# Half of batch 0's keys and queries by casting DMAs, its value globals by register DMAs, a new order of the first stage, and batch 1's data ahead of w_out

## Chip, core and metric

The kernel runs on one core of one Trainium2 chip. The metric is the device time of one execution in microseconds (us). Before the change four runs gave a median of 332.36 us (331.63 to 333.47).

## What is computed

A windowed attention with eight global tokens, and behind it a two-layer network with a squared ReLU. q, k, v are (8 batches, 8 heads, 576 tokens, 64), in fp32.

```python
scores = scale * np.matmul(q, k.transpose(0, 1, 3, 2))
mask = np.abs(pos[:, None] - pos[None, :]) <= 32
mask = mask | is_global[:, None] | is_global[None, :]
scores = np.where(mask, scores, -1000000000.0)
attn = softmax(scores)                       # per query
x = (attn @ v) as (4608 tokens, 512)
out = relu(x @ w_in) ** 2 @ w_out            # 512 -> 2048 -> 512
```

## The kernel before

**Tiles.** Two heads make a pair, so a batch has four pairs. Keys lie in five tiles of up to 120 tokens, each with the 8 global keys ahead of them (`kt`, 128 columns a tile); queries lie in four groups of 144 tokens, each followed by the 8 global queries (`qt`, 608 columns). A batch's queries are worked in two halves of 304 columns. For a pair and a half, PE computes scores for the tiles that the window touches, ACT the exponential (`weights`, L648), PE the weighted sum of values and the sum of weights (`outputs`, L672), ACT the reciprocal as exp(-ln) (`finish_outputs`, L704 and L705), and DVE the product into `xT` (L732), the network's input with features on partitions. The results of the global queries are put together in `global_outputs` and copied into their columns by `scatter` (L751), eight copies at positions that DVE reads from registers (`load_columns`, L741).

**Batch 0** is the start of the kernel, and its data have a way of their own. SP loads k and q pair by pair as fp32 (`fetch_tokens`, L107; tiles `stk`, `stq`), DVE or ACT casts them (`cast_tokens`, L449; tile `nat0k`, `nat0q`), PE transposes them with the identity and picks the global rows by a product with a one-hot matrix (`transposed`, L471 and L483), and DVE and ACT copy the results from PSUM to `kt` and `qt` (`tr_k`, `tr_q`, L493 to L510). The half-0 mask is built of a band (`ub`) and of row indicators (`rows`) by `mask_natural` (L250, L256), corrected at the global positions (`mask_globals_matmul`, L267; `mask_globals`, L284), and added to the scores as the first product of their PSUM group (`mask_added`, L292; `mask_first`, L625). Half 1 multiplies by the mask after the exponential (L652). GpSimd makes the constants (identity, band, token numbers) before it issues its first DMA (v, L114). The global rows of v for batch 0 come from v itself: a product with a one-hot matrix (`v_globals`, L457), an ACT copy (L459) and a DVE copy into row 0 to 7 of `vb[0]` (L460). Those of batches 1 and 2 are fetched by SP with DMAs at register addresses (`fetch_globals`, L375; tile `grows`), and put in place by `globals_in_place` (L382 to L385).

**Order.** Each engine works its instructions in the order of the program, which is written out by hand. After the index list (`indices`) and the one-hots come pair 0's transposes, then a loop in which pair i+1 is transposed before pair i's scores, with the exponential behind them; then the outputs of half 0 of all pairs; then half 1. `keep_warm(n)` puts n products of zeros (L201) into PE's order. From there the network's units are woven in: `take(n)` issues n of the units in a list. A unit of the first layer for a half of batch 0 (`mm1_half`, L543) is 8 products, a unit of the second (`mm2`, L587) is 4. `SCHED` says how many go where: h0 to h3 and p0 to p2 before batch 1, and three numbers for each pair of batch 1 (`unit`, L865: behind the scores, between the two output groups, at the end). Later batches have fixed numbers.

**DMA queues.** POOL's order is v of batch 0, w_in (L784, four DMAs), w_out (L799, four), k and q of batch 1 (cast on the way, tiles `natk`, `natq`), v of batch 1 (`fetch_values`), and then the scratch copies of batch 2 (L419), which SP transposes by DMA (L431). A POOL DMA waits for the one eight places ahead of it. SP's order is batch 0's k and q, then the 24 DMAs of `fetch_globals`, then the copies of `value_globals` (L440).

`SCHED` before:

```python
SCHED = dict(h0=0, w=4, h1=2, h2=2, h3=0, p0=3, p1=1, p2=2, b1=((2, 1, 2), (1, 1, 2), (1, 1, 2), (1, 1, 2)))
```

Of the kernel before, what the change touches and what calls it, by code (L numbers as in the profile page):

```python
# [17 lines left out]
KT = 120  # L18
NT = 5
# [23 lines left out]
SCHED = dict(h0=0, w=4, h1=2, h2=2, h3=0, p0=3, p1=1, p2=2, b1=((2, 1, 2), (1, 1, 2), (1, 1, 2), (1, 1, 2)))  # L43
# [4 lines left out]
def kernel(  # L48
# [63 lines left out]
    def fetch_values(b, x, hs=slice(0, H)):  # L112
        back = NG if b == 0 and x else 0
        pool.dma_start(  # L114
            out=vb[b][NG - back : NG + KN[x], x, 2 * hs.start : 2 * hs.stop : 2],
            in_=v[b, hs, x * KT - back : x * KT + KN[x]].rearrange("h s d -> s h d"),
        )

    act.dma_start(out=g64, in_=global_idx.unsqueeze(0))
    for hp in range(NHP):  # L120
        for nm in "kq":
            fetch_tokens(nc.sync, nm, 0, hp)
    act.preload_act_table_set("natural_log_exp_and_others")

# [6 lines left out]
    pidx = sbt("pidx", [P, 4], I32)  # L131
    nc.gpsimd.iota(pidx, pattern=[[0, 4]], base=0, channel_multiplier=1)
    icb = sbt("icb", [P, 4], I32)
    nc.gpsimd.iota(icb, pattern=[[2 * H * S, 4]], base=2 * H * S, channel_multiplier=0)
    ig = sbt("ig", [P, NG], FP32)
    nc.gpsimd.iota(
        ig, pattern=[[1, NG]], base=0, channel_multiplier=0, allow_small_or_imprecise_dtypes=True,
    )

    U0 = 48  # L140
    UN = 208
    ub = [sbt(f"ub{i}", [P, UN], FP16) for i in range(2)]
    nc.gpsimd.memset(ub[0], 1.0)
    for base, cu, cm in (
        (-8, 0, 1), (window + U0 - 8, -1, 1), (window - U0 + 8, 1, -1),
    ):
        nc.gpsimd.affine_select(
            out=ub[0], in_=ub[0], compare_op=ALU.is_ge, fill=0.0,
            base=base, pattern=[[cu, UN]], channel_multiplier=cm,
        )  # L150
    rows = sbt("rows", [P, 2], FP16)
    nc.gpsimd.memset(rows, 1.0)
    for col, base, cm in ((slice(0, 2), -8, 1), (slice(1, 2), KN[-1] + 7, -1)):
        nc.gpsimd.affine_select(
            out=rows[:, col], in_=rows[:, col], compare_op=ALU.is_ge, fill=0.0,
            base=base, pattern=[[0, col.stop - col.start]], channel_multiplier=cm,
        )
    nc.gpsimd.affine_select(
        out=ub[1], in_=ub[0], compare_op=ALU.is_ge, fill=0.0,
        base=KN[-1] + 7, pattern=[[0, UN]], channel_multiplier=-1,  # L160
    )

    tok = sbt("tok", [P, NT], FP32)
    nc.gpsimd.iota(
        tok, pattern=[[KT, NT]], base=-8, channel_multiplier=1,
        allow_small_or_imprecise_dtypes=True,
    )
    nc.gpsimd.affine_select(
        out=tok, in_=tok, compare_op=ALU.is_ge, fill=-1.0,
        base=-8, pattern=[[0, NT]], channel_multiplier=1,  # L170
    )
    tokp = sbt("tokp", [P, TJ], FP32)
    nc.gpsimd.iota(
        tokp, pattern=[[1, TJ]], base=0, channel_multiplier=TJ,
        allow_small_or_imprecise_dtypes=True,
    )
    identity = sbt("identity", [P, P], FP16)
    nc.gpsimd.memset(identity, 0.0)
    nc.gpsimd.affine_select(
        out=identity, in_=identity, compare_op=ALU.not_equal, fill=1.0,  # L180
        base=0, pattern=[[-1, P]], channel_multiplier=1,
    )
    for kt in kts:
        dve.memset(kt[:, 4, 8 + KN[4] : P], 0.0)
# [4 lines left out]

    def clear_tail(op, t):  # L190
        op(t[96:P, NT - 1, 0 : 2 * H : 2], 0.0)

    clear_tail(dve.memset, vb[0])
    for x in range(NT):
        fetch_values(0, x)
# [168 lines left out]
    grows = sbt("grows", [NG, 3, 2, H, D], FP32, bufs=2, tag="gt")  # L364
    grow = {nm: grows[:, i] for i, nm in enumerate("kqv")}
    g16s = {nm: sbt("g16s" + nm, [NG, 2, H, D], FP16) for nm in "kqv"}

    def fetch_globals():
        _, at = nc.values_load_multi_w_load_instructions(
            g32c[0:1, 0:NG], engines=[mybir.EngineType.SP], min_val=0, max_val=S - 1,  # L370
            skip_runtime_bounds_check_because="the values are clamped on the chip",
        )
        for nm in "kqv":
            for g in range(NG):
                nc.sync.dma_start(  # L375
                    out=grow[nm][g : g + 1],
                    in_=src[nm][1:3, :, ds(at[g], 1), :].rearrange("b h o d -> o b h d"),
                )
# [74 lines left out]
    def v_globals(hp, op1=None, op2=None):  # L453
        vs = vb[0][:, :, 4 * hp : 4 * hp + 4 : 2]
        gl = pst("mm", [P, 512])[0:NG, 0 : 2 * D]
        for t in range(NT):
            nc.tensor.matmul(gl, oh[:, t, :], vs[:, t], start=(t == 0), stop=(t == NT - 1))  # L457
        gvs = sbt("gvs", [NG, 2 * D], FP16, bufs=2)
        (op1 or act.copy)(out=gvs, in_=gl)  # L459
        (op2 or dve.tensor_copy)(  # L460
            out=vs[0:NG],
            in_=gvs.rearrange("p (h d) -> p h d", d=D).unsqueeze(1).to_broadcast((NG, NT, 2, D)),
        )

    def transposed(nm, i, tag):
        b, hp = divmod(i, NHP)
        tr = pst(tag, [P, 1024], FP16)
        for j in range(TJ):
            n = TP + NG if (b and j == TJ - 1) else TP
            if b == 0:  # L470
                nc.tensor.transpose(  # L471
                    tr[:, TP * j : TP * j + n], nat0[(nm, hp)][:, j, :], identity[0:n, 0:n]
                )
            for e in range(2) if b else ():
# [5 lines left out]
        if b == 0:  # L480
            gl = tr.bitcast(FP32)[:, 384 : 384 + NG]
            for j in range(TJ):
                nc.tensor.matmul(  # L483
                    gl, nat0[(nm, hp)][:, j, :], ohp[0:TP, j, :],
                    start=(j == 0), stop=(j == TJ - 1), skip_group_check=True,
                )
# [175 lines left out]
    def outputs(i, half, et, tag, wins, columns=False):  # L662
        b, hp = divmod(i, NHP)
        acc = pst(tag, [P, 2, 512])
# [3 lines left out]
        for n, (t, so, c0, w) in enumerate(wins[half] if columns else ()):  # L668
            o = c0 - half * BANKC
            for x in range(2):  # L670
                for e in range(2):
                    nc.tensor.matmul(  # L672
                        acc[D * e : D * e + D, x, o : o + w],
# [3 lines left out]
        for e in () if columns else range(2):  # L677
            for n, (t, so, c0, w) in enumerate(wins[half]):
# [3 lines left out]
                    acc[:, e, o : o + w], vtf[:, t, vo : vo + P], et[:, e, so : so + w],  # L682
                    start=(n == 0), stop=(n == nw - 1), skip_group_check=True,
                )
        return acc
# [12 lines left out]
    def finish_outputs(i, half, acc, columns=False):  # L698
        b, hp = divmod(i, NHP)
        parts = PARTS[columns]  # L700
        av = acc[:, :, 0:BANKC].rearrange("p x (k c) -> p x k c", c=GRP)
        rec = sbt("rec", [P, 2, GTOK], FP32, bufs=2)
        for r, x, rs, xs in parts:
            act.activation(out=rec[r], in_=av[rs, xs, :, 0:GTOK], func=AF.Ln)  # L704
        act.activation(out=rec, in_=rec, func=AF.Exp, scale=-1.0)  # L705
        if b == 0:
            if half == 0:
                if hp == 0:
                    gsum[0] = sbt("gs", [P, NHP, 2, NG], FP32, bufs=2)
                dve.tensor_reduce(  # L710
                    out=gsum[0][:, hp], in_=av[:, :, :, GTOK:GRP].rearrange("p e k g -> p e g k"),
                    axis=AX.X, op=ALU.add,
                )
# [3 lines left out]
        else:  # L717
            if hp == 0 and half == 0:
                gsum[b] = sbt("gsh", [P, 2, NHP, 2, NG], FP32, bufs=2)
            dve.tensor_reduce(  # L720
                out=gsum[b][:, half, hp], in_=av[:, :, :, GTOK:GRP].rearrange("p e k g -> p e g k"),
                axis=AX.X, op=ALU.add,
            )
# [7 lines left out]
        for r, x, rs, xs in parts:  # L731
            dve.tensor_tensor(  # L732
                out=xT[r, hp, x0 : x0 + HS].rearrange("p (k x) -> p k x", k=2),
                in0=av[r, x, :, 0:GTOK], in1=rec[r], op=ALU.mult,
# [25 lines left out]
    def transposes0(hp):  # L760
# [3 lines left out]
    index_base()  # L764
    keep_warm(6)
    mask_natural(0)
    gb = indices()
    fetch_globals()
    keep_warm(4)
    one_hots(gb)  # L770
    act.copy(
        out=vb[0][0:NG, 0, 0 : 2 * H : 2], in_=idle[0:NG].rearrange("p (h d) -> p h d", d=D)
    )
    mg = mask_globals_matmul(0)
    cast_tokens(dve.tensor_copy, "k", 0)
    cast_tokens(act.copy, "q", 0)
    mask_globals(mg, 0)
    transposes0(0)
    mask_added(0)
    scs = {0: mask_first(0, "sc")}  # L780
    for nm in "kq":
        cast_tokens(dve.tensor_copy, nm, 1)
    for i in range(4):
        pool.dma_start(out=w_in[:, :, ts(i, 512)], in_=wv[:, :, ts(i, 512)])  # L784

    ets = {}
    for i in range(NHP):
        if i + 1 < NHP:
            transposes0(i + 1)
            scs[i + 1] = mask_first(0, pair_tag[(i + 1) % 2])  # L790
        scores(i, 0, None, WIN, scs[i])
        ets[i] = weights(0, scs[i], WIN, added=True)
        if i + 2 < NHP:
            for nm in "kq":
                cast_tokens(dve.tensor_copy, nm, i + 2)
        keep_warm(1)
    gather_index()
    for j in range(4):
        pool.dma_start(out=w_out[:, ts(j, 4), :], in_=wo[:, ts(j, 4), :])  # L799
    mask_natural(1)  # L800
    columns()
    clear_ones(dve.memset, vb[0])
    load_columns(0)
    mg = mask_globals_matmul(1)
    v_globals(0)
    v_globals(1)
    for i in range(NHP):
        acc = outputs(i, 0, ets[i], pair_tag[i % 2], WIN, columns=True)
        if i + 2 < NHP:
            v_globals(i + 2)  # L810
        finish_outputs(i, 0, acc, columns=True)
        if i == 0:
            mask_globals(mg, 1)
        keep_warm(1)
    scatter(0, 0)
# [8 lines left out]
    half1(0)  # L824
    half1(1)
    act.copy(out=xT[:, :, XOFF + 256 : XOFF + HS], in_=xT[:, :, 256:HS])
    for i in range(0, NHP, 2):
        for nm in "kq":
            fetch_tokens(pool, nm, 1, i, 2)
    vb[1] = sbt("vb1", [P, NT, 2 * H, D], FP16)  # L830
    clear_tail(dve.memset, vb[1])
    for part in (1, None):
        load_columns(part)
    for x in range(NT):
        fetch_values(1, x)
# [45 lines left out]
    for hp in range(NHP):  # L881
        unit(NHP + hp, SCHED["b1"][hp], NHP + hp + 1 if hp + 1 < NHP else None)
        if hp == 1:
            clear_ones(dve.memset, vb[1])
# [47 lines left out]
```

The softmax here doesn't subtract the row's maximum and nothing guards it: scores larger than these inputs give would overflow.

## Time and profile before

| | |
|---|---|
| median of the runs | 332.36 us |
| profiled execution: time / span | 332.9 us / 331.2 us |
| busy: PE, DVE, ACT, POOL | 319.3, 224.3, 212.8, 107.3 us |
| first expert product (L543) | at 29.61 us |
| first scores of batch 2 | at 70.41 us |
| mean granted TensorE clock | 0.989 of full |

A line of the timeline begins with the start in us and the duration; then engine, line, operation, output and inputs, their shapes, the count, and, in brackets, how long the engine had been idle before and what ended that. A row of a stage gives each engine's busy time in it. A row of waits gives who waited for whom, the sum in us, how often, and the longest. "Granted clock" is TensorE's rate as a share of full speed. Durations on PE are those of pipelined products and can overlap.

### The profile page before, as it was taken

How to read it: one execution, taken by the hardware profiler on the slowest of the kernel's cores; microseconds unless marked ns; L12 is line 12 of the kernel's file. 1: busy time of each engine (PE TensorE's matmuls, PEld its weight loads, DVE VectorE, ACT ScalarE, POOL GpSimd, SP SyncE). 2: the span in 40 equal slices, each digit the busy share in tenths (PEclk: the TensorE clock that was granted, in tenths of full speed). 3: DMA queues.
4: the chain of work that ended last, by engine and by line, in shares of the span. 5: the costliest groups of instructions: out<-in, count | busy, mean ns of one | idle time of the engine just before them, and what ended most of it. 6: DMA issues, size and time to landing. Idle time of an engine off the chain costs nothing.

```text
span 331.2 us, 6785 instructions
## 1 busy us (share of the span) xinstructions
PE 319.3 (96%) x2393; PEld 167.0 (50%) x2393; DVE 224.3 (68%) x610; ACT 212.8 (64%) x425; POOL 107.3 (32%) x140
## 2 busy tenths in 40 slices
PE   7987999999999999999999999999999999999996
PEld 2665874445554545455545554554555444444444
DVE  6677985788768875887588757775887585323421
ACT  4577857659953995499549953995499536404700
POOL 8822486008900692078006930590000000000000
PEclk9599999999999999999999999999999999999999
DMA  7999999946999199999952999999410001011012
GB/s 202 196 205 205 204 160 144 141 138 74 135 144 203 17 133 150 176 110 141 153 112 56 125 119 136 177 145 155 104 65 1 32 34 63 0 65 63 1 46 83
DMA packets 148876, 38.20 MB, mean 115 GB/s; under 512 B 136818, under 2 KB 144362, under 8 KB 148842
## 3 DMA queue, kind: packets, MB, share of 16 engines
q0 software_dynamic: 104624, 17.37, 69.5%
q1 hardware_dynamic: 44072, 20.26, 31.3%
q8 instruction: 19, 0.31, 0.4%
q10 hardware_dynamic: 146, 0.13, 0.1%
q14 instruction: 15, 0.12, 0.1%
HBM read 37.36 MB, written 17.05 MB: 164 GB/s over the span
## 4 chain that ended last, share of the span: by engine, by line
PE 52%; ACT 23%; DVE 13%; issue 6%; DMA 4%; POOL 1%; DVEq 0%; ACTq 0%; POOLq 0%
PE mm L587 21%; PE mm L524 10%; ACT rl L529 8%; ACT et L648 7%; PE tr L587 5%; ACT rec L704 4%; PE mm L543 3%; DMA qb<-scr_q 3%; PE tr L524 3%; DVE xT L732 3%; ACT rec L705 2%; DVE et L652 2%; PE sc L681 2%; DVE gt L530 1%; DVE xT L751 1%
## 5 line engine op out<-in xcount | busy, mean ns | idle before, releaser
L587 PE MATMUL mm<-w_out,gt 128*128 128x512 f16 x448 | 104.9, 379 | 0.0
L524 PE MATMUL mm<-xT,w_in 128*128 128x512 f16 x384 | 90.8, 379 | 0.5 <-DVE xT L751 0.5
L587 PEld LDWEIGHTS <-gt 128*128 128x128 f16 x560 | 52.2, 98 | 58.1
L524 PEld LDWEIGHTS <-w_in 128*128 128x128 f16 x512 | 47.4, 98 | 54.0 <-issue 1.1
L529 ACT ACTIVATE rl<-mm 128x512 f16<-128x512 f32 x96 | 55.1, 600 | 26.4 <-PE mm L524 25.8
L530 DVE TENSOR_TENSOR gt<-rl 128x512 f16<-128x512 f16 x128 | 52.2, 424 | 16.6 <-ACT rl L529 14.4
L648 ACT ACTIVATE et<-sc 128x880 f16<-128x880 f32 (+1 forms) x32 | 28.9, 904 | 43.7 <-PE sc L639 43.7
L652 DVE TENSOR_TENSOR et<-et,mask 128x880 f16<-128x880 f16 x60 | 36.7, 615 | 26.3 <-ACT et L648 26.1
L114 POOL DMA_DIRECT2D vb<-in_v_dram x40 | 41.7, 1602 | 9.0 <-DMA w_out<-in_moe_w_out_dram 7.6
L524 PE MATMUL tr<-xT,w_in 128*128 128x512 f16 x128 | 32.9, 380 | 0.0
L564 DVE COPY ot<-mm 128x512 f32<-128x512 f32 (+1 forms) x29 | 19.7, 680 | 17.5 <-PE mm L587 15.8
L732 DVE TENSOR_TENSOR xT<-sc,rec 64x288 f16<-64x288 f32 (+1 forms) x56 | 25.5, 455 | 8.8 <-ACT rec L705 8.4
L890 POOL COPY pin<-gsh 1x1 f32<-1x1 f32 x5 | 0.9, 177 | 90.7 <-DVE gsh L720 90.7
L705 ACT ACTIVATE rec<-rec 128x288 f32<-128x288 f32 x64 | 28.3, 443 | 2.0
L648 ACT ACTIVATE et<-acc 128x880 f16<-128x880 f32 (+1 forms) x32 | 29.0, 907 | 0.5 <-PE acc L639 0.5
L732 DVE TENSOR_TENSOR xT<-acc,rec 64x288 f16<-64x288 f32 (+1 forms) x56 | 25.5, 455 | 5.1 <-ACT rec L705 4.7
L681 PEld LDWEIGHTS <-vb 128*128 128x128 f16 x288 | 21.4, 98 | 12.6 <-issue 2.0
L419 POOL DMA_DIRECT2D scr_k<-in_k_dram x30 | 26.6, 1091 | 1.9 <-issue 1.3
L704 ACT ACTIVATE rec<-sc 64x288 f32<-64x288 f32 (+1 forms) x56 | 22.8, 407 | 6.3 <-PE sc L681 4.2
L587 PE MATMUL tr<-w_out,gt 128*128 128x512 f16 x112 | 25.3, 379 | 0.0
L419 POOL DMA_DIRECT2D scr_q<-in_q_dram x24 | 24.9, 1586 | 0.3 <-issue 0.2
L704 ACT ACTIVATE rec<-acc 64x288 f32<-64x288 f32 (+1 forms) x56 | 22.6, 404 | 1.9 <-PE acc L672 1.1
(135 smaller groups left out, 301.8 us busy)
## 6 DMA issues: line engine op xcount, KB each, us to landing
out_dram<-ot SPq DMA_DIRECT2D x35, 256.0 KB
vb<-in_v_dram POOLq DMA_DIRECT2D x29, 120.0 KB, 10.7
scr_q<-in_q_dram POOLq DMA_DIRECT2D x24, 144.0 KB, 5.8
scr_k<-in_k_dram POOLq DMA_DIRECT2D x24, 120.0 KB, 4.5
w_in<-in_moe_w_in_dram POOLq DMA_DIRECT2D x4, 512.0 KB, 12.5
w_out<-in_moe_w_out_dram POOLq DMA_DIRECT2D x4, 512.0 KB, 18.2
stk<-in_k_dram SPq DMA_DIRECT2D x4, 288.0 KB
stq<-in_q_dram SPq DMA_DIRECT2D x4, 288.0 KB
```

The costliest lines, as they stand in the source:

```text
L114: pool.dma_start(out=vb[b][NG - back : NG + KN[x], x, 2 * hs.start : 2 * hs.stop : 2], in_=v[b, hs, x * KT - back : x * KT + KN[x]].rearra ...
L419: pool.dma_start(out=scr[(nm, b % 2)][x * pitch + off : x * pitch + off + hi - lo].rearrange("s (h d) -> s h d", d=D), in_=src[nm][b, :, l ...
L524: nc.tensor.matmul(ph, w_in[:, t, u * P : (u + 1) * P], xT[:, t, XOFF + c * TC : XOFF + (c + 1) * TC], start=(t == 0), stop=(t == NDM - 1),)
L529: nc.scalar.activation(out=rl, in_=ph, func=AF.Relu)
L530: nc.vector.tensor_tensor(out=gts[c][:, u, :], in0=rl, in1=rl, op=ALU.mult)
L587: nc.tensor.matmul(po, gts[c][:, f, m * P : (m + 1) * P], w_out[:, f, :], start=(f == 0), stop=(f == NFF - 1),)
L648: act.activation(out=et[:, :, 0:W], in_=sc[:, :, 0:W], func=AF.Exp, bias=0.0, scale=scale)
L652: dve.tensor_tensor(out=et[:, :, 0:W], in0=et[:, :, 0:W], in1=mask[:, MB[half] : MB[half] + W].unsqueeze(1).to_broadcast((P, 2, W)), op=AL ...
L681: nc.tensor.matmul(acc[:, e, o : o + w], vtf[:, t, vo : vo + P], et[:, e, so : so + w], start=(n == 0), stop=(n == nw - 1), skip_group_che ...
L704: act.activation(out=rec[r], in_=av[rs, xs, :, 0:GTOK], func=AF.Ln)
L705: act.activation(out=rec, in_=rec, func=AF.Exp, scale=-1.0)
L732: dve.tensor_tensor(out=xT[r, hp, x0 : x0 + HS].rearrange("p (k x) -> p k x", k=2), in0=av[r, x, :, 0:GTOK], in1=rec[r], op=ALU.mult,)
```

## The change

- k and q of pairs 0 and 1 of batch 0 still come by SP as fp32 and are cast on chip. Those of pairs 2 and 3 are cast by two POOL DMAs into `natk` and `natq`, are transposed head by head (24 transposes and 24 one-hot products per pair instead of 12 and 12), and need no cast.
- GpSimd makes only three ramps before its first DMA; DVE makes identity, band, row indicators and token numbers of them (`constants`, `last_rows`). v of batch 0 is issued behind the two casting DMAs.
- The value globals of batch 0 are fetched by eight SP DMAs at register addresses, ahead of the 24 others, and copied by DVE (fp32 to fp16) into `vb[0]`. Products, ACT copies and the clearing of the global rows are gone.
- The order: pair 0's transposes ahead of the mask's correction; the column indices and a register load (`columns`, `load_columns(0)`) right behind them; pair 1's casts and transposes; then scores and exponentials of pairs 0 and 1; the half-1 mask; transposes of pairs 2 and 3; their scores and exponentials; then the four outputs of half 0, whose PSUM banks are taken from three tags in turn (two single banks `mm`, or `sc`, or `acc`). The scatter of half 0 moves between half 1's scores of pair 0 and pair 1. The number of zero products changes, and six stand behind half 1's first scores.
- POOL's order is now v, w_in, k and q of batch 1, v of batch 1, w_out. k and q of heads 4 to 7 of batch 1 wait until PE has transposed those of batch 0.
- `clear_ones` for `vb[0]`, `index_base` and `gather_index` move into batch 1's units. The numbers in `SCHED` change.
- The sum over groups of global queries in `finish_outputs` is two reductions of one bank each instead of one over both, in all batches.

```diff
-SCHED = dict(h0=0, w=4, h1=2, h2=2, h3=0, p0=3, p1=1, p2=2, b1=((2, 1, 2), (1, 1, 2), (1, 1, 2), (1, 1, 2)))
+SCHED = dict(wa=6, w0=6, w1=5, w2=0, w3=3, w4=1, h0=0, w=4, h1=3, h2=2, h3=0, p0=0, p1=2, p2=2, b1=((2, 1, 2), (2, 1, 2), (1, 1, 2), (2, 0, 4)))
...
-    for hp in range(NHP):
+    for hp in range(2):
         for nm in "kq":
             fetch_tokens(nc.sync, nm, 0, hp)
...
+    dif = iota("dif", [P, UN], FP32, 1, 0, -1)
+    tokp = iota("tokp", [P, TJ], FP32, 1, 0, TJ)
+    tok = iota("tok", [P, NT], FP32, KT, -8, 1)
+    for nm in "kq":
+        fetch_tokens(pool, nm, 0, 2, 2)
+    for x in range(NT):
+        fetch_values(0, x)
...
+    def constants():
+        dve.tensor_scalar(
+            out=identity, in0=dif[:, 0:P], scalar1=0.0, scalar2=None, op0=ALU.is_equal
+        )
+        dve.tensor_scalar(
+            out=ub[1], in0=dif, scalar1=float(U0 - window - NG), scalar2=None, op0=ALU.is_ge
+        )
+        dve.scalar_tensor_tensor(
+            out=ub[0], in0=dif, scalar=float(U0 + window - NG), in1=ub[1],
+            op0=ALU.is_le, op1=ALU.mult,
+        )
...
+        for g in range(NG):
+            nc.sync.dma_start(
+                out=gv0[g : g + 1], in_=v[0, :, ds(at[g], 1), :].rearrange("h o d -> o h d")
+            )
...
+    def v_globals(hp, op):
+        op(
+            out=vb[0][0:NG, :, 4 * hp : 4 * hp + 4 : 2],
+            in_=gv0[:, pair(hp)].unsqueeze(1).to_broadcast((NG, NT, 2, D)),
+        )
...
-                dve.tensor_reduce(
-                    out=gsum[0][:, hp], in_=av[:, :, :, GTOK:GRP].rearrange("p e k g -> p e g k"),
-                    axis=AX.X, op=ALU.add,
-                )
+                for x in range(2):
+                    dve.tensor_reduce(
+                        out=gsum[0][:, hp, x], in_=av[x][:, :, GTOK:GRP].rearrange("p k g -> p g k"),
+                        axis=AX.X, op=ALU.add,
+                    )
...
+    constants()
+    one_hots(gb)
     cast_tokens(dve.tensor_copy, "k", 0)
     cast_tokens(act.copy, "q", 0)
+    mask_natural(0)
+    transposes0(0)
+    mg = mask_globals_matmul(0)
     mask_globals(mg, 0)
+    columns()
+    load_columns(0)
+    cast_tokens(dve.tensor_copy, "k", 1)
+    cast_tokens(dve.tensor_copy, "q", 1)
     mask_added(0)
+    keep_warm(SCHED["w3"])
+    tr_k(1, tail=act.copy, last=act.copy)
+    keep_warm(SCHED["w4"])
+    tr_q(1, act.copy)
...
+    half0(0)
+    half0(1)
+    last_rows()
+    mask_natural(1)
+    mg = mask_globals_matmul(1)
+    mask_globals(mg, 1)
...
+    keep_warm(SCHED["w2"])
+    for hp in range(2, NHP):
+        tr_k(hp)
+        tr_q(hp, act.copy)
...
+    for x in range(NT):
+        fetch_values(1, x)
+    for j in range(4):
+        pool.dma_start(out=w_out[:, ts(j, 4), :], in_=wo[:, ts(j, 4), :])
+    for i in range(NHP):
+        v_globals(i, dve.tensor_copy)
+    half0(2)
+    half0(3)
+    half0_out(0, "mm")
+    half0_out(1, "sc")
+    half0_out(2, "acc")
+    half0_out(3, "mm")
...
+    half1(0)
+    scatter(0, 0)
+    keep_warm(SCHED["wa"])
+    half1(1)
...
-        if hp == 1:
-            clear_ones(dve.memset, vb[1])
+        if hp < 2:
+            clear_ones(dve.memset, vb[hp])
+        else:
+            (index_base, gather_index)[hp - 2]()
```

## Prediction

> **What bounds the kernel now.** I read the page's head, then busy time by stage, then the chain of waits and the timeline of the first 30 us, then the waits of the stage behind it. The profiled execution took 332.9 us, 0.5 above the median of 332.36; its span is 331.2 us. By stage (columns: us, busy of PE, weight loads, VectorE (DVE), ScalarE (ACT), GpSimd (POOL), granted TensorE clock, DMA share, GB/s):
>
> ```profile
> 0.00:29.60 29.60, 23.91 (x309) 14.49 (x309) 21.24 (x89) 17.32 (x47) 17.41 (x37) 0.88 1.27 201
> 29.60:72.30 42.70, 41.06 (x483) 26.36 (x481) 32.12 (x90) 30.04 (x60) 17.16 (x19) 1.00 1.61 165
> 72.30:331.20 258.90, 254.38 (x1604) 126.14 (x1603) 170.89 (x432) 165.47 (x319) 72.69 (x84) 1.00 0.89 97
> ```
>
> From 29.6 us, when the first expert matmul (L543) starts, PE is occupied for all but 6.2 us. That work is the same after the change, so what can move is (a) the moment 29.6 and (b) the 1.64 us without PE work up to 72.3. Before 29.6 PE's busy time holds 21 matmuls on zeros (L201); latency rules there, in three parts. ACT shows them: the exponentials of half 0 (L648), then the reciprocals (L704, L705).
>
> ```profile
> 12.02 0.93 ACT L648 ACTIVATE et<-sc 128x912 f16<-128x912 f32 x1 [0.57 <-PE sc L639]
> ...
> 18.61 0.97 ACT L648 ACTIVATE et<-acc 128x912 f16<-128x912 f32 x1
> 19.42 0.41 ACT L459 CAST gvs<-mm 8x128 f16<-8x128 f32 x2
> 21.22 0.26 ACT L459 CAST gvs<-mm 8x128 f16<-8x128 f32 x1 [1.39 <-PE mm L457]
> 21.39 0.40 ACT L704 ACTIVATE rec<-sc 128x288 f32<-128x288 f32 x1
> ...
> 25.32 0.44 ACT L705 ACTIVATE rec<-rec 128x288 f32<-128x288 f32 x1
> ```
>
> Part one: the fourth exponential ends at 19.58. Part two: the value globals (PE L457, ACT L459, DVE L460) stand in front of every output, so ACT idles 1.39 us, its first reciprocal begins 1.8 us later, and four pairs that take 0.8 each (L704 then L705, 0.42 apart) take 4.4. Part three, on DVE: last xT done at 26.31, then
>
> ```profile
> 26.35 1.86 DVE L751 COPY xT<-gx 128x4 f16 x8
> 27.91 1.14 DVE L652 TENSOR_TENSOR et<-et,mask 128x880 f16<-128x880 f16 x2
> ```
>
> and the two output groups on PE: 3.3 us to 29.61. In part one the chain of waits is mostly PE, and its granted clock by the microsecond is
>
> ```profile
> 9.00:10.00 1.00, 0.74 (x15) 0.92 1.10 266
> 10.00:11.00 1.00, 1.00 (x14) 0.50 1.30 235
> ...
> 16.00:17.00 1.00, 1.00 (x22) 0.67 1.21 194
> 17.00:18.00 1.00, 0.94 (x15) 1.00 1.31 206
> ```
>
> that is, half rate from 9.9 to 16.4.
>
> **The change, part by part.**
>
> *To the first cast.* GpSimd's 4.66 us of constants become three iotas, and DVE computes them after the indices (constants). DVE now stands at the index list: its landing is not shown (DVE read it at 4.33 without a wait; the DMA was issued at 0.82). Between 3.1 and 4.3 I take 3.1, since the first keys, 288 KB issued in the same moment on SP, had landed by 5.34. Four small index operations 0.6 (4.33 to 4.94), twelve constants about 1.35 (an estimate from 0.39 for 128x8, 0.64 for 128x456, and 0.07 to 0.16 for tiny ones), one-hots 0.46: the first cast starts at 5.6 instead of 5.34; at the other end 6.2. The mask copies (1.05) move behind it and are hidden by the two transposes (0.55 each); if PE were faster than that they would show. First kt copy ends at 8.0, as before (7.99).
>
> *Pair 1 goes ahead of the first exponential.* On DVE the four column clamps (0.61, L221 and L222) and a register load now stand between that copy and pair 1's casts. The load is a row:
>
> ```profile
> L741 DVEq TENSOR_LOAD <-g32a x1: 842/842/842, 18.4 to 18.4; - x1
> ```
>
> At 18.4 it ran beside memsets; here everything queued on DVE waits: the casts, far, kt1, and through them PE's pair 1. Pair 1's q cast ends at 8.0+0.6+0.85+0.55+0.8 = 10.9 instead of 9.83. Then at half clock PE: one zero matmul 0.5, transposes 0.9, mask 0.8, scores 0.5: the first exponential starts at about 13.5 instead of 12.02. From there ACT has four exponentials at 0.85, four mask corrections 0.55 and pairs 2 and 3's qt at 0.85 each: 5.7; before, 7.56 with three pairs and kt tails. I add 1.1 for PE's 48 transposes and 48 one-hot products of pairs 2 and 3 (12 natk transposes took 0.45, as long as 6 merged ones at 0.43), which wait for the mask's PSUM bank. Fourth exponential ends 20.3: **+0.7**. With the clock full throughout it is 1.5 earlier.
>
> *Fewer casts, DMA casts.* Four DVE casts (0.54 to 0.90) leave, already counted. [...] The row: with v's casts issued from 4.66, the rate stayed at SP's 244 to 273 GB/s until 10 us, and POOL was still waiting for a v DMA at 13.4, so SP kept most of the engines. I take 0, and keep 0.55.
>
> *Value globals by register DMAs.* Removed: 20 matmuls, four ACT copies, four DVE copies on the path. Added: 8 small DMAs at the head of SP's list; by the existing ones (0.75 to 0.89 each, issued from 5.9) they are out by 13 and land by about 15, and 24 others move back from 25.8 to 32, needed near 38. The four DVE copies (f32 now, 0.45 to 0.5) run under the exponentials. ACT goes straight from exponential to reciprocals. The bound passes to DVE: two reductions in place of one (0.19; I take 0.3 the two), xT 0.46, four times, and 0.9 for global_outputs: 3.9 behind the first logarithm (0.4): last xT at 20.3+4.35 = 24.65, against 26.31: **-1.65**. Clear_ones (1.37) leaves this stage too.
>
> *Part three.* DVE now multiplies et of pair 0, scatters, multiplies pair 1: 0.55+1.86+0.57, output 0.55 = 3.5, against 3.3. The six zero matmuls (1.35) fit under the scatter; had it gone, they would cost that. First expert matmul at 24.65+3.5 = 28.15 against 29.61: **-1.45**.
>
> *Behind it.* Gone is the scatter's wait, since four units stand behind it instead of one or two:
>
> ```profile
> PE acc L639 <- DVE xT L732: 1.0, 3, 0.4
> PE mm L524 <- DVE xT L751: 0.4, 1, 0.4
> ```
>
> -0.35. New: with p0=0 batch 1's first transpose comes right behind half 0's units, but ACT copies its global rows (0.62, L382) only after their relus: +0.3 (0 to 0.6). Clear_ones of vb0 and the index arithmetic (1.37, about 1.6) enter batch 1's units on DVE; they lie under two units (1.9), scores 0.5 and exponential 0.9, as vb1's clearing did at 58.80; without that cover they would cost 0.4 to 1.4. The split reductions (56 more, 0.19 each) run beside the 0.44 of L705: 0, between -0.1 and +0.3 per launch, since PE idles there 1.0 in all. Batch 1's keys land before w_out: no PE wait named them, so no gain. w_out's last chunk moves from 38.6 (a POOL wait released by it) to about 45 (batch 1's 1.77 MB ahead of it at 0.2 MB per us is 8.9, less 2 for the f32 staging that shrinks and the earlier start); its first chunk is needed at 48, as before (48.15), the last at 51. Sum of this stage: **-0.1** (-0.6 to +1).
>
> Total -1.55 of the profiled 332.9, 331.3; from the median, **330.8**.
>
> **The rivals.** *The clock holds* because zero matmuls now stand between the transposes: -1.5 more, 329.3. For it: half rate began in a stretch where PE was 0.40 and 0.69 busy; against: PE still waits there from 8.5 to 10.
>
> *Hidden anyway*: late index list (+0.6), shared DMA (+0.55) and the 0.3 eat the gain and the first expert matmul stays near 29.5: 332.1. That includes the case that the casting DMAs do not spare anything, since the last exponential is later, not earlier.
>
> [...]
>
> **How the numbers follow.** Sum as worked out 0.46 (own range 330.0 to 331.7, nearly half of it faster by over 0.5%), clock holds 0.22, hidden 0.20, slower 0.12, most of it beyond 0.5%. About 0.5%, or 1.7 us, is what a measurement of this kernel tells from no change. Range 328.9 to 332.9.
>
> **What would show it.** Right: fourth exponential ends at 20 to 20.5, reciprocals dense behind it, last xT near 24.7, first L543 matmul near 28.2, no wait of PE before the matmuls of batch 2. Wrong: a first exponential after 14.5 or half clock past 17 (part one); ACT gaps between reciprocals (part two); PE waiting for w_out or for batch 1's global rows by more than 0.6.

## The result: no difference, and the profile after

The kernel after took 333.14 us (median of 42 runs, 330.14 to 337.38); the kernel before, on the same chips, 332.69 us (63 runs). The ratio is 1.000, with a 95% interval of 0.998 to 1.002: no difference, where 330.8 was predicted. Ratios leave out runs over 1.5% above the fastest of their kernel, which in the kernel after are eight runs with a mean granted clock of 0.988 or less, so the medians of all runs stand beside the ratios below.

The profiled execution took 334.35 us, span 332.4, mean granted clock 0.984. Its stages, in the columns of the stage rows of before, cut at the same events (first expert product, first product of network chunk 1):

```profile
0.00:28.83 28.83, 23.53 (x340) 14.30 (x341) 19.87 (x90) 15.80 (x39) 16.13 (x29) 0.82 1.30 189
28.83:74.08 45.25, 41.00 (x484) 26.45 (x481) 36.31 (x110) 28.58 (x59) 16.59 (x20) 1.00 1.51 158
74.08:332.40 258.32, 254.52 (x1604) 125.98 (x1603) 173.99 (x483) 166.73 (x320) 72.74 (x84) 1.00 0.88 97
```

The first stage is 0.78 us shorter than before's 29.61, the second 2.55 longer than its 42.69 with the same PE work (41.0 busy), the third 0.58 shorter: 1.2 more in all. Two things have to be found: why the first stage gains only half of the 1.45 forecast, and where the second loses 2.55.

ACT's timeline of the first stage shows what held and what did not:

```profile
12.23 0.93 ACT L648 ACTIVATE et<-sc 128x912 f16<-128x912 f32 x1
...
20.14 0.93 ACT L648 ACTIVATE et<-acc 128x912 f16<-128x912 f32 x1 [0.46 <-PE acc L639]
21.18 0.41 ACT L708 ACTIVATE rec<-mm 128x288 f32<-128x288 f32 x1
21.62 0.44 ACT L709 ACTIVATE rec<-rec 128x288 f32<-128x288 f32 x1
```

The 1.39 us gap ahead of the reciprocals is gone. But from the first exponential to the end of the fourth it is 8.84 us, 7.56 before. The clock rows (second number from the left: PE busy; third from the right: granted clock) say why:

```profile
8.00:9.00 1.00, 0.00 (x0) 0.00 (x0) 0.37 (x1) 0.35 (x4) 0.72 (x1) 1.00 1.20 208
...
11.00:12.00 1.00, 1.00 (x17) 0.49 (x15) 0.85 (x5) 0.68 (x3) 0.20 (x1) 0.65 2.28 152
...
21.00:22.00 1.00, 1.00 (x34) 1.00 (x32) 0.35 (x2) 0.86 (x4) 0.13 (x1) 0.73 1.27 204
```

Half rate lasts from about 11.3 to 21.5, 10.2 us; in before it was 6.8 by the same rows. And ahead of it PE stood still for a whole microsecond. PE's timeline shows that gap and the one behind it, DVE's what was waited for:

```profile
6.82 0.82 PE L198 MATMUL tr<-idle 128*128 128x512 f16 x3
9.24 0.43 PE L468 MATMUL mm<-identity,nat0k 96*128 96x96 f16 x6 [1.60 <-DVE nat0k L451]
...
10.59 0.43 PE L468 MATMUL mm<-identity,nat0q 96*128 96x96 f16 x6 [0.55 <-DVE nat0q L451]
```

```profile
8.63 0.56 DVE L451 CAST nat0k<-stk 96x768 f16<-96x768 f32 x1 [0.79 <-DMA stk<-in_k_dram]
9.97 0.56 DVE L451 CAST nat0q<-stq 96x768 f16<-96x768 f32 x1 [0.79 <-DMA stq<-in_q_dram]
```

```profile
L747 DVEq TENSOR_LOAD <-g32a x1: 845/845/845, 7.7 to 7.7; - x1
```

The key cast's wait is put down to a DMA, but DVE's register load (7.7 to 8.55) covers the same 0.79; the query cast has nothing else than the DMA before it. In before both casts ran without a wait:

```profile
8.46 0.54 DVE L449 CAST nat0k<-stk 96x768 f16<-96x768 f32 x1
8.93 0.90 DVE L449 CAST nat0q<-stq 96x768 f16<-96x768 f32 x1
```

In the second stage two waits of PE are new. In each row stand their sum, how often, and the longest; each sum is larger than that of any wait of PE that stood there before (1.0):

```profile
PE mm L543 <- DVE xT L757: 1.9, 1, 1.9
PE sc L676 <- DMA vb<-g16sv: 1.7, 3, 0.8
```

The first is for the half-1 scatter: its eight copies took 3.65 us (the line stands with the run "POOL held"), 1.66 in before:

```profile
36.60 1.66 DVE L751 COPY xT<-gx 128x4 f16 x8
```

The second is for batch 1's global values, which DVE casts (L385) behind that scatter at 42.01 instead of 40.26, and SP then copies in five DMAs.

### The profile page after: what moved, and what is told of

The parts are those of the page before. It is cut to its first block, busy times and chain, and to the rows that moved or that the text cites. A ratio compares the mean times of both kernels' runs of the same rounds, so it can differ in the third digit from the quotient of the medians.

```text
span 332.4 us, 6909 instructions
## 1 busy us (share of the span) xinstructions
PE 319.0 (96%) x2424; PEld 166.7 (50%) x2424; DVE 230.2 (69%) x682; ACT 211.1 (64%) x416; POOL 105.5 (32%) x132
## 4 chain that ended last, share of the span: by engine, by line
PE 80%; DVE 9%; DMA 4%; ACT 3%; issue 2%; SPq 1%; DVEq 0%
PE mm L524 25%; PE mm L587 25%; PE tr L524 9%; PE tr L587 6%; PE sc L685 3%; PE acc L685 3%; DVE xT L757 2%; PE sc L639 2%; DMA stq<-in_q_dram 2%; DVE xT L738 2%; PE acc L639 2%; DMA vb<-g16sv 2%; PE mm L543 1%; ACT rec L709 1%; ACT rec L708 1%
## 6 DMA issues: line engine op xcount, KB each, us to landing
w_out<-in_moe_w_out_dram POOLq DMA_DIRECT2D x4, 512.0 KB, 10.8
```

## The experiments

**Theory 1:** the early start is given back in these two waits. **Theory 2:** the half clock is what decides, and PE's idle gap before pair 1's transposes brings it. **Theory 3:** the gap itself comes from the casting DMAs, which hold up pair 1's data, and from the register load.

All ratios are to the kernel before on the same chip. "Full clock" counts the executions with a mean granted clock of 0.999 or more, with their median (of all executions, the profiled ones too, but for four that took over 340 us). The last two columns are from one profiled execution each: the moment of the first expert product, and from there to the first product of chunk 1.

| kernel | median us | ratio (95%) | full clock, their median | L543 at | to chunk 1 |
|---|---|---|---|---|---|
| before | 332.4 to 332.9 | 1 | 117 of 196, 332.25 | 29.61 | 42.69 |
| after | 333.14 | 1.000 (0.998 to 1.002) | 8 of 44, 331.13 | 28.83 | 45.25 |
| unit numbers of before | 332.72 | 1.001 (0.998 to 1.004) | 7 of 14, 331.56 | 28.11 | 45.16 |
| globals cast early | 334.57 | 1.006 (1.004 to 1.008) | 2 of 16, 333.01 | 26.51 | 47.91 |
| POOL held | 332.83 | 1.000 (0.997 to 1.003) | 7 of 14, 331.81 | 28.02 | 43.31 |
| units and early | 336.34 | 1.014 (1.009 to 1.018) | 0 of 6 | 27.82 | 46.37 |
| zero products | 331.59 | 0.997 (0.995 to 0.999) | 12 of 21, 331.28 | 24.99 | 43.74 |
| none of them | 335.26 | 1.005 (1.002 to 1.009) | 0 of 18 | 29.34 | 43.64 |
| POOL's start late | 333.46 | 1.001 (0.998 to 1.004) | 1 of 13, 332.38 | 27.16 | 44.86 |
| zeros, POOL held | 331.52 | 0.998 (0.996 to 1.001) | 7 of 14, 331.40 | 25.72 | 43.31 |
| zeros, load moved | 333.98 | 1.002 (0.998 to 1.005) | 6 of 14, 331.94 | 27.97 | 45.64 |
| before, zero products | 333.05 | 1.002 (0.999 to 1.004) | 4 of 14, 332.09 | 28.53 | 43.62 |
| before, new POOL order | 334.45 | 1.003 (1.000 to 1.007) | 9 of 14, 333.38 | 27.22 | 44.19 |
| zeros, load moved, both waits mended | 331.16 | 0.996 (0.994 to 0.998) | 18 of 22, 331.03 | 26.04 | 42.60 |
| zeros, load moved, POOL late | 330.00 | 0.992 (0.990 to 0.994) | 8 of 13, 329.93 | 25.04 | 45.02 |
| zeros, w_out first again | 333.99 | 1.003 (1.000 to 1.005) | 2 of 22, 331.76 | 26.01 | 47.87 |
| all mended | 329.99 | 0.992 (0.990 to 0.995) | 10 of 13, 329.69 | 24.27 | 42.84 |
| load moved, POOL late | 329.56 | 0.990 (0.987 to 0.993) | 4 of 6, 329.01 | 24.24 | 43.55 |

**The waits behind the start**

*Unit numbers of before*

```diff
-h1=3, h2=2, h3=0, p0=0, p1=2, p2=2, b1=((2, 1, 2), (2, 1, 2), (1, 1, 2), (2, 0, 4))
+h1=2, h2=2, h3=0, p0=3, p1=1, p2=2, b1=((2, 1, 2), (1, 1, 2), (1, 1, 2), (1, 1, 2))
```

> The kernel after, with the unit numbers of before (h1=2, p0=3, p1=1, p2=2, and batch 1's numbers). Theory 1 (the early start is given back in waits behind it, the first of them, 1.9 us, made because only three half-0 units stand between the last half-1 output and the half-1 units that need the scatter): with h1=2 four units of half 0 stand there, 0.9 us more cover, so PE's wait for the scatter at L757 shrinks from 1.9 to about 1.0 and the time falls by about 0.9 us (332.2); the wait for batch 1's global values stays 1 to 2. Rival (half clock in part one is all of it): no change from the kernel after, 333.1.

The wait went from 1.9 to 1.4 only, since the scatter still took 3.34 us, and the stage is as long as in after (45.16). The unit numbers are not what makes it long.

*Globals cast early*: `globals_in_place()` moves ahead of `half1_out(3)`.

> The kernel after, with batch 1's global rows cast (globals_in_place) ahead of the last half-1 output instead of behind the half-1 scatter; their DMAs have landed by then. Theory 1 (waits behind): DVE's cast moves from 42.0 to about 35, the copies of value_globals start some 6 us earlier, and PE's 1.7 us of waits before batch 1's first outputs are gone; but DVE and ACT have 1.5 us more in front of the last half-1 product, so the scatter wait grows by up to 0.8: time lower by 0.9 to 1.7, 331.5 to 332.2. Rival (half clock): no change, 333.1.

The wait for the global values went, but PE's wait for the scatter rose to 3.7 and the stage to 47.91: slower. DVE's three casts (1.5 us) now stood ahead of the last product and the scatter, the scatter still took 3.45, and in this profile the clock was at half rate from 37.9 to 44.7.

*POOL held*

```diff
     value_globals(1)
+    pool.tensor_copy(out=pin[0:1], in_=g16s["v"][0:1, 0, 0, 0:1])
     globals_to_scratch(2)
     tokens_to_scratch(2)
```

> The kernel after, with one 1x1 POOL copy that reads the cast global values ahead of the scratch copies of batch 2, so that POOL issues them only after DVE's half-1 scatter. Theory 1a (the scatter's copies took 414 ns instead of 176 because POOL was issuing DMAs beside them): the scatter takes 1.7 us again instead of 3.7, PE's wait for it falls from 1.9 to about 0.2 and the wait for the global values from 1.7 to about 0.5; time lower by about 2, 331. Theory 1b (it is the unit order, or DVE's queue, and the slow copies are a chance of that execution): scatter still about 3.5, time within 0.5 of 333.1. Rival (half clock): 333.1.

The timelines of DVE and POOL in after, and then in this kernel:

```profile
36.70 3.65 DVE L757 COPY xT<-gx 128x4 f16 x8
...
36.28 3.65 POOL L421 DMA_DIRECT2D scr_k<-in_k_dram  x4
```

```profile
35.88 1.65 DVE L757 COPY xT<-gx 128x4 f16 x8
...
40.21 2.70 POOL L421 DMA_DIRECT2D scr_k<-in_k_dram  x3
```

In after POOL issues four DMAs in the very time of the scatter, whose copies take 176 to 862 ns (median 414); with POOL quiet, all eight take 175 to 177 ns and PE no longer waits. So the scatter is slow when it coincides with POOL's DMA issues, as theory 1a said. The runs show only the coincidence and its end, not what in the hardware makes it. In the time it is not seen: at full clock 331.81 against 331.13. In its profile the stage is 1.9 us shorter than in after, but from chunk 1 on it takes 263.2 us, 258.3 in after; PE waits there for the DMAs that transpose later batches' queries, as it doesn't in after:

```profile
PE sc L639 <- DMA qb<-scr_q: 3.1, 2, 2.3
```

Whether the held DMAs make this wait, or chance, is open.

*Units and early*: both of the first two edits.

> The kernel after, with the unit numbers of before and batch 1's global rows cast ahead of the last half-1 output. Theory 1: both waits shrink, by 0.9 and by 1.7, less up to 0.8: time lower by 1.8 to 2.6, about 331. Rival (half clock): 333.1.

Wrong sign: 336.34. The profile shows the reason of the second run again (scatter 3.16 us, PE's wait 2.3), and none of the six executions had full clock; how much each took isn't separated.

**The clock**

*Zero products*: `w3=9, w4=3` instead of 3 and 1.

> The kernel after, with nine instead of three zero products ahead of pair 1's key transposes and three instead of one ahead of its query transposes, so that PE works through its gaps of 1.60 and 0.55 us, in which it waits for pair 1's data. Theory 2 (the half clock): of the runs of the kernel after, 8 of 44 have a mean granted clock of 0.999 or more, at 331.1 us, and 12 of 44 one below 0.989, at 335.4; before has 20 of 37 at 0.999 or more. If the idle gaps bring the half clock, the share at full clock rises to half or more and the median falls by about 1.5, to 331.5. Theory 1 (waits behind): no change, 333.1. [...]

*None of them*: `w3=0, w4=0`.

> The kernel after, without the zero products ahead of pair 1's key and query transposes (four fewer), so that PE idles some 2.4 us there. Theory 2 (half clock): full-clock runs become rare, mean clock falls below 0.989, median up by 1 to 2, to 334.5. Theory 1: no change, 333.1.

The three kernels differ in nothing but zero products: with 0, 4 and 12 of them the mean clock over all runs is 0.980, 0.991 and 0.998, and the medians 335.3, 333.1 and 331.6. Within the kernel after, the 8 runs at full clock have 331.13, the 12 below 0.989 have 335.37. So the clock moves the time, and zero products in these gaps move the clock, as theory 2 said; whether it is the gap or the lack of products, a later run tells. The profile with none has half rate from 9.5 to 23.2, from the end of a gap of 2.18 us; the one with twelve has none. The rows of their first stages, without and with:

```profile
0.00:29.34 29.34, 24.43 (x336) 15.40 (x336) 20.01 (x90) 15.86 (x39) 18.06 (x31) 0.77 1.31 193
0.00:24.99 24.99, 21.17 (x348) 12.50 (x348) 19.16 (x90) 15.62 (x39) 15.65 (x28) 1.00 1.30 189
```

*Before, zero products*: `keep_warm(3)` ahead of `mask_added(0)` and one between pair 1's key and query transposes.

> The kernel before with four more zero products in PE's idle gaps of its first stage (three ahead of the first mask product, 0.90 us, one ahead of pair 1's query transposes, 0.26). Theory 2 (half clock): it too has full clock in most runs, its mean clock rises from 0.997 to 0.999, and its median falls by 0.3 to 0.6, to 332.0; what the change is worth at equal clock is then the difference from the kernel after with zero products (331.6), 0.4 to 0.9. [...]

Nothing gained: 4 of 14 at full clock. In its profile the first 26 us were at full clock, and half rate came at 26.8, beside a gap of 1.08 us (PE waiting for a half-1 mask product), for 3.4 us. So the clock can fall later than near 9 us, here still ahead of the first expert product (28.53), and in the second stage too, as in this profile of the run with the load moved (below), where the wait for the scatter costs its 1.85 us and then 3.4 us of half rate; first PE's timeline, then the clock rows:

```profile
39.54 3.52 PE L543 MATMUL mm<-xT,w_in 128*128 128x256 f16 x16 [1.85 <-DVE xT L757]
```

```profile
39.00:40.00 1.00, 0.46 (x3) 0.34 (x4) 0.97 (x5) 0.00 (x0) 0.97 (x2) 0.72 1.24 210
40.00:41.00 1.00, 1.00 (x6) 0.69 (x5) 0.97 (x3) 0.00 (x0) 0.12 (x1) 0.50 1.24 206
```

*Zeros, POOL held*

> The kernel after, with both the zero products of PE's gaps (nine and three) and the 1x1 POOL copy that keeps the scratch copies of batch 2 behind the half-1 scatter. Theories 1 and 2 together: more full-clock runs, and no PE wait for the half-1 scatter (1.9): about 330.5, 2 below the kernel before. If only the clock counts: 331.5.

Half rate was gone in its profile and the wait for the scatter too, but the time is that of zero products alone. In that kernel the early start had already moved the scatter (32.86 to 34.70) mostly ahead of POOL's scratch copies (from 34.29; POOL's issues ahead of them wait for DMAs): little was left to mend.

**What makes the gap**

*POOL's start late*

```diff
     one_hots(gb)
+    pin0 = sbt("pin0", [P, 1], FP32)
+    pool.tensor_copy(out=pin0[0:1], in_=oh[0:1, 0, 0:1])
+    for nm in "kq":
+        fetch_tokens(pool, nm, 0, 2, 2)
+    for x in range(NT):
+        fetch_values(0, x)
```

(and the same four lines out of the place above).

> The kernel after, with POOL's first DMAs (the casting ones of pairs 2 and 3, and v) held by a 1x1 copy until the one-hots are there, so that they start at 4.6 us instead of 1.5, as v's did before. Theory 3 (the casting DMAs take the DMA engines from pair 1's data on SP): DVE's two waits of 0.79 us for stk and stq are gone, pair 1's query cast ends near 9.2 instead of 10.5, the first exponential begins near 11.3, and PE idles 1.5 less there, so that the clock is full in more runs; but pairs 2 and 3's keys and queries, which landed at 10.5 and 12.4, land near 14 and 15.5, and PE waits for them, about 0.5 to 1 before their transposes: time lower by 0 to 1. If POOL's DMAs did not hold SP's: waits unchanged, time up by 0.5 to 1.

Neither: POOL's first DMA now began at 5.07 (1.47 in after) and no DMA wait was left, but the clamps and the register load held the key cast until 8.81, PE's gap was 1.94 and the time the same:

```profile
8.81 0.96 DVE L447 CAST nat0k<-stk 96x768 f16<-96x768 f32 x1 [0.33 <-DVE g32b L215]
```

*Zeros, load moved*: `columns()` and `load_columns(0)` go behind `mask_globals(mg, 1)`; `w3=6, w4=3`.

> The kernel after with zero products in PE's gaps (six and three), and with the column clamps and DVE's register load moved from between pair 0's key copies and pair 1's casts to behind the half-1 mask, where DVE idles. If the load's 0.85 us and the clamps' 0.9 hold pair 1 up: its key cast starts near 7.0 to 7.6 instead of 8.64 and the first exponential near 10.6 instead of 11.65; against the kernel with zero products alone (331.6, first expert product at 25.0) lower by 0.5 to 1.2, 330.7. If the wait was for pair 1's data all the same: the cast stays at 8.4 to 8.6, the query cast at 9.2 to 10, and the time at 331.6.

Neither, again: without the load the key cast came at 9.23 and the query cast at 10.93, and now nothing but the DMA stood before them. DVE's waits of that stage:

```profile
DVE nat0k L451 <- DMA stk<-in_k_dram: 2.3, 1, 2.3
DVE nat0q L451 <- DMA stq<-in_q_dram: 1.1, 1, 1.1
```

*Zeros, load moved, POOL late*: both edits.

> The kernel after with zero products (six and three), the register load moved behind the half-1 mask, and POOL's first DMAs held by a 1x1 copy until the one-hots are there (4.6 us instead of 1.5). It differs from the run with the load moved by that hold alone, and nothing but pair 1's data can now hold its casts. Theory 3 (the casting DMAs share the engines with SP's loads): DVE's waits for stk and stq, 2.27 and 1.15 us in that run, fall below 0.3, and the casts start near 7.6 and 8.3; pairs 2 and 3's data land some 3 us later, so that PE waits for natk or natq, 0.5 to 2 us in all; time 331 to 332.5. If SP's loads are late for another reason: the waits stay above 1.

Both waits are gone, the casts start at 7.54 and 8.01, and the data of pairs 2 and 3 are still in time: 330.00, the first version clearly faster than before. From the run with the load moved it differs by the hold alone, and at full clock it is 2.0 faster (331.94 to 329.93). So each of the two causes hid the other, and theory 3 holds: either of them, the early DMAs or the register load, can make the gap (1.48 us with the load moved, 1.94 with POOL late). *Load moved, POOL late*, with the zero products of after (3 and 1):

> The kernel after with the register load moved and POOL's first DMAs held until 4.6 us, and with its own zero products (three and one). If the half clock comes from PE's idle time and not from a lack of zero products as such: pair 1's data now come in time, the gap before its transposes shrinks from 1.6 to about 0.5, most runs have full clock and the time is 330 to 330.5. If the products are needed all the same: mean clock below 0.993, 331.5 to 332.5.

The first fence is DVE's timeline of pair 1's casts, the second the row of the first stage:

```profile
6.71 0.55 DVE L447 CAST nat0k<-stk 96x768 f16<-96x768 f32 x1
7.44 0.65 DVE L447 CAST nat0q<-stq 96x768 f16<-96x768 f32 x1 [0.18 <-DMA stq<-in_q_dram]
```

```profile
0.00:24.24 24.24, 19.95 (x341) 12.19 (x341) 20.05 (x90) 15.36 (x39) 15.19 (x28) 1.00 1.27 182
```

With after's four zero products PE has no gap above 0.2 us before 10 us, and the clock is full throughout the stage: 329.56, ratio 0.990 (0.987 to 0.993), faster than both kernels; four of six executions had full clock. So the zero products aren't needed once the gap is closed: it is the gap, not a lack of them.

**The order of POOL's DMAs**

*Before, new POOL order*: in the kernel before, batch 1's keys, queries and values ahead of w_out, nothing else.

> The kernel before with one part of the change alone: batch 1's keys, queries and values issued on POOL ahead of w_out instead of behind it. Theory 1a (POOL's scratch copies fall on the half-1 scatter because of this order): the scatter, 1.66 us before, takes 2.5 or more, PE waits for it and the time rises by 0.5 to 1.5, to 333.5. If the order alone does not bring them together (the f32 staging is still double, and POOL starts its DMAs at 4.7): scatter 1.7, no PE wait for w_out, within 0.3 of 332.5.

The time rose a little (ratio 1.003, its interval from 1.000; 333.38 at full clock against 332.25), but not by the way expected: the half-1 scatter took 1.81 us, and PE waited 1.86 us until 70.05, ahead of batch 2's scores. The profile names DVE's scatter for that wait. In before the same scores began at 70.41, ahead of that scatter (70.59 to 72.25), so they don't need it; the DMA transposes that they do need moved their last packets until 69.24, until 67.52 in before, and are the likelier cause. This profiled execution took 331.84, less than most, so it doesn't show what the order costs.

*Zeros, w_out first again*: the kernel after with the two groups of DMAs in the order of before.

> The kernel after with zero products in PE's gaps (nine and three), and with w_out ahead of batch 1's keys, queries and values on POOL again, as before the change. If the new order costs in it what it cost alone in the kernel before (1.3 at full clock): 330.2, 1.3 below the kernel with zero products alone. If batch 1's keys and values, now behind w_out, come too late for a start 2 us earlier: PE waits for natk or vb, 1 to 3 us, and the time is 332 to 334.

```profile
PE tr L472 <- DMA natk<-in_k_dram: 4.4, 1, 4.4
```

Slower by 2.4 than zero products alone (1.9 by the ratios): with a start at 26.0 batch 1's keys come too late behind w_out, and half rate follows that wait, from 40.3 to 43.7. This part of the change is needed by the others, and alone it costs a little.

**All together**

*Zeros, load moved, both waits mended*: besides, SP fetches the global rows in the order v, k, q, `g16s["v"]` is cast ahead of `half1_out(2)`, and POOL's held copy reads `g16s["k"]`.

> All mended together: the kernel after with zero products in the gaps, the register load moved, the global values of batches 1 and 2 fetched ahead of keys and queries and cast before the third half-1 output, and POOL's scratch copies held until the global keys are cast, behind the half-1 scatter. Theories 1 and 2: no PE wait for the scatter (1.9) nor for the global values (1.7), full clock in most runs: 329.5 to 330.5, 2 to 3 below the kernel before. If the later scratch copies then hold batch 2 up, or DVE's earlier cast delays the half-1 outputs: 331 to 331.6, no better than zero products alone.

As theories 1 and 2 wanted in the stage (42.60 us, PE's wait for the scatter 0.4), less in the time: 331.16. At full clock it is 0.9 below the same kernel without the two mended waits. The median is 2.8 below; 18 of 22 executions had full clock, and 6 of 14 there, which suggests that the two waits had cost clock as well. Its first stage is the same program as in the run with the load moved, but in this profile pair 1's keys were there at 7.45 instead of 9.23, and PE had no gap above 0.2 us near 9 us:

```profile
7.45 0.62 DVE L450 CAST nat0k<-stk 96x768 f16<-96x768 f32 x1 [0.49 <-DMA stk<-in_k_dram]
```

So with POOL's DMAs early the landing varies from execution to execution, and one profile doesn't tell how often the gap comes.

*All mended*: the same with POOL's late start.

> The fastest so far (zero products six and three, register load moved, POOL's first DMAs held until 4.6 us), and with it the global values of batches 1 and 2 fetched and cast first and POOL's scratch copies held behind the half-1 scatter. The two waits behind the early start were worth 0.9 at full clock without the late DMAs (331.94 against 331.03): 329.1. If the early start is bounded by something that doesn't move with it (batch 2's transposes, out at 64 us in all fast runs), no gain: 330.0.

329.99: no better than without the two mended waits, but better than without the hold (at full clock 329.69 against 331.03). Chunk 1 came at 67.11, earliest of all, and then PE waited 2.0 us in two waits for batches' transposed queries (0.8 in before, none in the kernel without the two):

```profile
PE sc L634 <- DMA qb<-scr_q: 2.0, 2, 1.8
```

From chunk 1 on this profile has 261.1 us, that of the kernel without the two mended waits 258.4: the 2.95 us by which chunk 1 comes earlier are nearly all given back, 2.0 of them in these waits. The DMA chain that was expected to bound it, batch 2's transposes (issued until 64.6 here, until 63.3 to 66.3 in all profiles), isn't it: the longer wait, 1.8 us, is at 101.8, for batch 3. As in "POOL held", the later scratch copies may have a part in it.

## Why the prediction was wrong

**The step that failed first is the clock's.** The sum took half rate from the row of before ("half rate from 9.9 to 16.4"; the row, 0.67, makes it 16.7) and gave the case of a longer one 0.12. In the profiled execution half rate lasted to 21.5, and from the first exponential to the end of the fourth it took 8.84 us where 6.8 were forecast; the ten profiles with full clock there took 5.9 to 6.5. **The second is *Behind it*:** -0.1 was forecast, +2.55 measured.

In spans the profiled execution misses by 2.75 us (1.2 slower instead of 1.55 faster). The exponentials at half rate make 2.04 of that and the stage behind 2.65; 1.27 came back ahead of the first exponential, 0.58 in the third stage, 0.1 between.

Over all executions the clock weighs more, by this estimate. In 36 of 44 executions of the kernel after the clock was not full, in 79 of 196 of before; at full clock the two are 331.13 and 332.25, 1.1 faster where 1.55 was forecast, and the mean over all runs (333.38 and 332.69) is 0.7 slower. So the clock takes about 1.8 us, and only some 0.45 of the miss is left for the rest. The estimate rests on full clock: at a mean clock of 0.993 to 0.995 the medians are 332.44 (15 executions) and 332.64 (48), at 0.988 to 0.990 333.60 (9) and 333.75 (11), a gain of 0.2 at most. Where half rate stood in those isn't recorded.

Of the rivals, "slower" (0.12), a longer half rate, had the right effect in the profiled execution: half to 21.5. The transposes of pairs 2 and 3, in a row without zero products, don't bring it by themselves: with the gap closed, the same row of transposes kept full clock (1.00 over the first stage of "load moved, POOL late"); only in "POOL's start late" did half rate begin at 15.9, behind these transposes and 6.1 us behind the gap, which leaves their part in it open. "Hidden anyway" (332.1) is nearest in time, by luck: of its three terms the delay by POOL's DMAs was there, the late index list was not, and batch 1's global rows cost far more than the 0.3.

**Behind the longer half rate stands a term set to zero**, *Fewer casts, DMA casts*: "I take 0". The runs show a delay: pair 1's keys landed at 7.45 and 9.23 with POOL's DMAs from 1.5 on, and by 6.71 with POOL held to 5.07. I had read POOL's slow v DMAs in before as a sign that SP wins; there POOL started 3 us later, when by the rates of the microsecond rows (20, 238, 298 and 253 GB/s up to 4.66) 0.7 of pairs 0 and 1's 1.18 MB were in. The 0.55 kept beside the 0, which is a term of "hidden anyway" as well, is shown by no run; in its place they show that with the load moved the hold is worth 2.0 at full clock (331.94 to 329.93), and that beside its own time the delay makes the gap (1.48 us) that half rate follows.

**Point by point, in the profiled execution.**

| step | forecast | measured |
|---|---|---|
| first cast | 5.6 | 4.54 |
| pair 1's query cast ends | 10.9 (its terms add up to 10.8) | 10.53 |
| first exponential | 13.5 | 12.23 |
| fourth exponential ends | 20.3 | 21.07 |
| from there to the last xT product | 4.35 | 4.32 |
| to the first expert product | 3.5 | 3.44 |
| stage behind it, change | -0.1 | +2.55 |

- *To the first cast*: 1.06 us earlier than forecast, since the index list was there at 1.98. (The zero products ahead of 29.6 in before are 22, not 21.) *Pair 1 ahead of the first exponential*: the register load's 0.84 was right and lay on the path as said.
- *Value globals by register DMAs* and *part three*: both right to 0.1.
- *Behind it*: wrong. The gain forecast from the scatter's wait came (0.7 less, 1.0 to 0.3), and nothing was lost to w_out. I had put batch 1's global rows at 0.3 on ACT; it was 1.7 on the value side, DVE's cast and SP's five copies. The scatter's 1.9 was not thought of: that moving w_out behind batch 1's data puts POOL's scratch copies beside it. With both mended the stage is 42.60, as before, but at full clock the time moves by 0.2 to 0.9, not 2.5; in one of the two profiles most of it goes to a later DMA wait.

What stays open: why one execution of the same kernel gets full clock and another does not (8 of 44 in the kernel after), why the gain at a clock short of full is 0.2 at most, why more zero products did not help the kernel before, and how much of the 1.9 and 1.7 reaches the end in the kernel after as it stands.

## What to carry to other kernels

Where PE waits in a latency-bound stage, look at the granted clock in the rows behind it: here half rate followed all seven gaps of 1.36 us or more near 9 us, and the gap's own length was the smaller part of its price (1.6 us, and 2.4 to 3.0 more from the first to the fourth exponential). Before DMAs are started earlier on a second queue, ask which transfer of the first queue is needed next; here holding the second queue back by 3.6 us and taking a 0.85 us register load out of one engine's way turned no gain into 1%. Two causes that cover the same wait must be removed together to see either.

## What was not expected of the hardware

- In the 18 profiles, all seven with a PE gap of 1.36 us or more near 9 us had half rate behind it, six of them within 2.3 us of its end, one 6.1 us behind (that one may have another reason). Of the eleven others, whose gaps there were 1.02 us at most, two had half rate in the first stage, before at 9.8 and before with zero products at 26.8. Of 24 gaps of 1 us or more between 20 and 80 us only four had it beside or right behind them.
- Between 6 and 86 us of the 18 profiles half rate came in 13 pieces: six of 3.4 us, two of 6.8, four of 10.2 and one of 13.6, none of a length between.
- Eight SBUF copies of 128x4 on DVE took 1.65 us with POOL quiet and, in six profiles, 3.2 to 3.65 us while POOL issued DMAs for most of it, single ones up to 862 ns instead of 176 (after). Squares of 128x512 on DVE kept their time beside such issues (424 ns at 51.9 and 53.8 in after, 417 and 419 with POOL quiet at 34.3 and 38.2 in before).
- Pair 1's keys landed at 7.45 us in one profiled execution and at 9.23 in another, in two kernels that are the same up to there.
